# Long convolution and its two adjoints: DFTs of 1024 points in place of 1023, overlap-add on the spectra in place of a second pair of inverse matrices

## The chip, the cores and the metric

The kernel runs on one core of a Trainium2 chip. A core has a matrix engine (PE, with its weight loads shown apart as PEld), a vector engine (DVE), an activation engine (ACT), GpSimd (POOL) and a sync engine (SP), each with a queue of its own that is worked off in order, and 16 DMA engines. The metric is the time of one execution on the device in microseconds (us). A profile is one execution with its instructions recorded; its span is the time from the first to the last of them.

## What is computed

One layer, forward and backward. With `xn` the layer norm of x (2048 x 576):

```python
K = einsum("dn,dnl,dn->dl", Cc, P, dB).real           # 576 kernels of 2048 taps
y = irfft(rfft(pad(xn.T)) * rfft(pad(K)))[:, :2048]   # causal convolution along the sequence
s = y.T + xn * Dskip
g = silu(ffn(xn))                                     # gated feed-forward, 576 -> 4608 -> 576
out = x + s * g
```

The reference returns `out` and the gradients of it for x and all parameters. With gs the gradient that reaches s, the convolution's backward needs two correlations: gK (of gs with xn), from which the gradients of the parameters of K follow, and the part of xn's gradient that comes from gs and K. Output 9 is the sum over the sequence of gs * xn.

## The kernel before

The work runs in stages, one behind another in the text: constants and layer norm (phase 1), the parameters (phase 2), the generation of K (`phase2_kgen`, 36 chunks of 16 columns), the convolution (`phase3_conv`), the feed-forward (phase 4), the two correlations (`phase5_scopeA`), the sums that make the parameter gradients (`param_sums`, again 36 chunks) and the feed-forward's backward (phase 6). A framework puts every engine's instructions in order by dependencies and a priority that follows the text, so that an instruction far down in the text may be queued early where its inputs and buffers are there; it adds the semaphores. Buffers come from pools: a pool with `bufs=2` has two places for each name, and a tile waits until the one before it in its place has been read for the last time. A pool that is opened later may lie where a closed one lay, and waits for its last readers.

The sequence of 2048 is cut into NB = 4 blocks of LS = 512. A block lies as KT = 4 tiles of 128 rows by D = 576 columns, and `dpieces` cuts the columns into two of 288 for PSUM. All of the convolution is done by blocks: `fwd_dft` (L508) turns a block into a real and an imaginary spectrum of 512 frequencies with matrices `Cf` and `Sf`, 8 PSUM groups of 4 matmuls for each piece, evicted by ACT. `cmac` (L523) multiplies two block spectra on DVE and adds to an accumulator, with 6 instructions of 2304 elements for a first product and 8 for another. The DFT has M = 1023 points, so a product of two blocks of 512 fits without wrapping, and 512 frequencies hold all of it.

The inverse of output block m has two parts: the first 512 outputs of its own product sum (`CiL`, `SiL`) and the tail of the previous block's (`CiPN`, `SiPN`, kept as `Yprev` or `Znext`). A group of one output tile and one piece therefore has 16 matmuls, 8 for the block at the edge. In `phase3_body` the products are `Yr`, `Yi` from a pool with two buffers; the epilogue on DVE (L629, L631) adds xn * Dskip, and `s_t` goes to `S_dram`. The spectra of xn and K are kept in DRAM (`UH_dram`, `KH_dram`) for the backward.

`phase5_scopeA` transforms gs, forms output 9 with a column of ones, loads the spectra of xn, computes gK by four blocks from the last to the first (L871, evicted by ACT to `gK` at L872), loads the spectra of K, and computes the other correlation in the same way (L906), with an epilogue on DVE that adds gs * Dskip and a store to `GXN_dram`. `build_dft_mats` (L462) makes the six matrices from the row and column numbers on DVE and ACT; it is called twice, at the head of phase 3 and at the head of phase 5. `param_sums` begins with a copy of gK and a copy of it times the position (`gKK`, L941 and L943).

Of the kernel before, what the change touches and what calls it, by code (L numbers as in the profile page):

```python
# [10 lines left out]
ACT = mybir.ActivationFunctionType  # L11
ALU = mybir.AluOpType
# [4 lines left out]
P = 128  # L17
# [43 lines left out]
class K:  # L61
# [368 lines left out]
    def gen_dft_rows(self, sb, out_c, out_s, tvals_col, col0, ncols, wcol=None, sin_sign=-1.0):  # L430
        nc, cfg = self.nc, self.cfg
        M = float(cfg.M)
        TWO_PI_S = 6.283184
        assert ncols <= self.irow.shape[1]
        prod = sb.tile([P, ncols], FP32, name="g_prod")
        nc.vector.tensor_scalar(out=prod[:], in0=self.irow[:, 0:ncols], scalar1=float(col0), scalar2=tvals_col,
                                op0=ALU.add, op1=ALU.mult)
        q = sb.tile([P, ncols], FP32, name="g_q")
        nc.vector.tensor_scalar(out=q[:], in0=prod[:], scalar1=1.0 / M, scalar2=MAGIC, op0=ALU.mult, op1=ALU.add)
        nc.vector.tensor_scalar(out=q[:], in0=q[:], scalar1=-MAGIC, scalar2=-M, op0=ALU.add, op1=ALU.mult)  # L440
        tau = sb.tile([P, ncols], FP32, name="g_tau")
        nc.vector.tensor_tensor(out=tau[:], in0=prod[:], in1=q[:], op=ALU.add)
        u = sb.tile([P, ncols], FP32, name="g_u")
        nc.vector.tensor_scalar(out=u[:], in0=tau[:], scalar1=1.0 / M, scalar2=MAGIC, op0=ALU.mult, op1=ALU.add)
        nc.vector.tensor_scalar(out=u[:], in0=u[:], scalar1=-MAGIC, scalar2=None, op0=ALU.add)
        fr = sb.tile([P, ncols], FP32, name="g_fr")
        nc.vector.scalar_tensor_tensor(out=fr[:], in0=tau[:], scalar=1.0 / M, in1=u[:], op0=ALU.mult,
                                       op1=ALU.subtract)
        A = sb.tile([P, ncols], FP32, name="g_A")
        nc.scalar.activation(out=A[:], in_=fr[:], func=ACT.Abs)  # L450
        if wcol is None:
            nc.scalar.activation(out=out_s, in_=fr[:], func=ACT.Sin, scale=sin_sign * TWO_PI_S)
# [42 lines left out]
    def dpieces(self):  # L495
        D = self.cfg.D
        if D <= 512:
            return [(0, D)]
        n = (D + 511) // 512
        w = (D + n - 1) // n  # L500
        out = []
        o = 0
# [895 lines left out]
```

## Time and profile before

| | us |
|---|---|
| median of 3 runs | 3275.29 (3269.64 to 3278.9) |
| profiled execution | 3264.63 |
| its span | 3262.9 |
| PE busy | 2197.4 (67%) |
| DVE busy | 1750.6 (54%) |
| ACT busy | 1424.8 (44%) |
| convolution, from the last tile of K to the first matmul of phase 4 | about 401 to 657 |
| phase 4 | about 657 to 1131 |
| correlations, to the first matmul of the parameter sums | about 1131 to 1550 |
| parameter sums and their end | about 1550 to 2148 |
| phase 6 | about 2148 to 3263 |

The profile is read from a page of the whole execution and from views of its trace: groups of instructions by line, the order of time, who waited for whom, the chain of work that ended last, and windows with each engine's busy time. An engine that is busy in a window does not have to be what sets its length; an idle one that others wait for can. "PEclk" is the share of full speed at which the matrix engine was clocked.

### The profile page before, as it was taken

The numbers are of one execution on the slowest core, as the hardware profiler recorded it, in microseconds if no ns is written. First come the engines' busy times: TensorE is split into PE (matmuls) and PEld (weight loads), VectorE is DVE, ScalarE is ACT, GpSimd is POOL, SyncE is SP. The second block draws the span as 40 slices with busy tenths as digits, with TensorE's granted clock in tenths as the row PEclk, the third lists the DMA queues.
The fourth block names the chain that finished last, engine by engine and source line by source line (L and its number), as shares of the span: only waits on it lengthen the run. The fifth ranks groups of instructions, "written<-read, shape, count | busy, mean of one in ns | idle before, by whom it ended". The sixth has DMA issues, their size and how long they took to land.

```text
span 3262.9 us, 43023 instructions
## 1 busy us (share of the span) xinstructions
PE 2197.4 (67%) x17602; PEld 1417.2 (43%) x17670; DVE 1750.6 (54%) x2690; ACT 1424.8 (44%) x1626; POOL 256.0 (8%) x504
## 2 busy tenths in 40 slices
PE   1556556499979854453444444169899999956999
PEld 1232235333337633331111111047677777744777
DVE  6586847734435657678777777734343444310222
ACT  2899752044431151001777667166555555500000
POOL 0000000021111000000000000022222222110000
PEclk7555578699989967676555555589999999977999
DMA  3100011186667510110000000075444444347442
GB/s 94 29 27 23 26 58 73 43 293 222 234 227 241 153 58 5 58 58 22 14 17 14 17 17 13 13 220 169 127 139 140 130 137 132 113 116 212 170 153 84
DMA packets 311752, 333.81 MB, mean 102 GB/s; under 512 B 113833, under 2 KB 271786, under 8 KB 308354
## 3 DMA queue, kind: packets, MB, share of 16 engines
q1 hardware_dynamic: 173914, 116.20, 12.2%
q0 software_dynamic: 33552, 109.15, 10.0%
q10 hardware_dynamic: 104088, 105.71, 9.9%
q8 instruction: 138, 2.26, 0.3%
q14 instruction: 60, 0.49, 0.0%
HBM read 163.94 MB, written 150.52 MB: 96 GB/s over the span
## 4 chain that ended last, share of the span: by engine, by line
PE 29%; DVE 21%; issue 18%; ACT 7%; DMA 5%; POOL 3%; SPq 3%; ACTq 0%; POOLq 0%; DVEq 0%
PE px L1283 8%; PE ph L1190 4%; DVE pr_q L1000 3%; PE dft_ps L516 3%; SPq L1095 3%; PE pgw L1231 2%; ACT S_q L302 2%; DMA out_dram<-gw 2%; PE inv_ps L627 2%; PE pT L996 2%; DVE S_all L1002 2%; PE gk_ps L871 2%; PE pgw L1219 2%; PE gu_ps L906 2%; ACT A_q L304 2%
## 5 line engine op out<-in xcount | busy, mean ns | idle before, releaser
L1283 PE MATMUL px<-w1T,ggc 128*128 128x288 bf16 x1152 | 237.3, 288 | 42.7 <-DMA w1T<-in_B_w_dram 42.7
L1231 PEld LDWEIGHTS <-xn_bf 128*128 128x128 bf16 x2304 | 228.4, 100 | 68.9 <-issue 38.6
L1283 PE MATMUL px<-w3T,guc 128*128 128x288 bf16 x1152 | 237.2, 288 | 28.3 <-DMA guc<-GU_dram 19.7
L1000 DVE TENSOR_TENSOR pr_q<-pT,pz 128x512 f32<-128x512 f32 x144 | 146.9, 1061 | 72.0 <-PE pT L996 72.0
L1234 DVE CAST gw<-pgw 128x256 bf16<-128x256 f32 x144 | 59.9, 423 | 233.2 <-DMA out_dram<-gw 137.4
L711 DVE CAST g_t<-pg 128x1024 bf16<-128x1024 f32 x72 | 88.2, 1225 | 179.8 <-ACT s_t L710 179.8
L703 PEld LDWEIGHTS <-wmB_w 128*128 128x128 bf16 x1152 | 107.2, 98 | 159.0 <-issue 41.2
L1287 DVE TENSOR_TENSOR gx<-px,gx 128x288 f32<-128x288 f32 x32 | 13.2, 453 | 293.0 <-PE px L1283 293.0
L1300 ACT ACTIVATE t<-gx 128x576 f32<-128x576 f32 x16 | 10.9, 683 | 362.9 <-DVE gx L1287 362.9
L996 PE MATMUL pT<-gKK,qr 128*128 128x32 bf16 x576 | 69.7, 233 | 145.8 <-DVE qr L990 145.8
L1219 PE MATMUL pgw<-go_o,h_n 128*128 128x288 bf16 x1152 | 165.7, 287 | 0.8
L1231 PE MATMUL pgw<-gg_n,xn_bf 128*128 128x256 bf16 x1152 | 138.8, 283 | 35.1 <-DVE gw L1234 35.1
L1190 PE MATMUL ph<-go_oT,w2T 128*128 128x512 bf16 x682 | 161.2, 380 | 1.4 <-ACT gh L1193 0.3
L747 PE MATMUL po<-w2res,hc 128*128 128x288 bf16 x1152 | 145.8, 288 | 17.9 <-DMA hc<-H_dram 17.9
L710 ACT ACTIVATE s_t<-pg 128x1024 bf16<-128x1024 f32 x72 | 73.7, 1023 | 166.2 <-PE pu L708 154.2
L1283 PEld LDWEIGHTS <-ggc 128*128 128x128 bf16 x1152 | 113.4, 99 | 73.0 <-issue 43.8
L703 PE MATMUL pg<-xnT,wmB_w 128*128 128x512 bf16 x561 | 137.2, 382 | 8.8 <-DMA S_dram<-s_t 5.9
L1283 PEld LDWEIGHTS <-guc 128*128 128x128 bf16 x1152 | 113.3, 98 | 59.1 <-DMA guc<-GU_dram 20.2
L1231 PE MATMUL pgw<-gu_n,xn_bf 128*128 128x256 bf16 x1152 | 137.5, 273 | 0.0
L703 PE MATMUL pu<-xnT,wmB_w 128*128 128x512 bf16 x562 | 136.4, 381 | 0.7
L996 PEld LDWEIGHTS <-qr 128*128 128x128 bf16 x576 | 63.9, 122 | 167.6 <-DVE qr L990 167.6
L747 PEld LDWEIGHTS <-hc 128*128 128x128 bf16 x1152 | 112.2, 99 | 48.1 <-issue 18.4
(361 smaller groups left out, 5273.0 us busy)
## 6 DMA issues: line engine op xcount, KB each, us to landing
U_dram<-u_t POOLq DMA_DIRECT2D x36, 512.0 KB, 3.1
G_dram<-g_t POOLq DMA_DIRECT2D x36, 512.0 KB, 4.1
H_dram<-h_t SPq DMA_DIRECT2D x36, 512.0 KB
hc<-H_dram SPq DMA_DIRECT2D x8, 2304.0 KB
gate<-G_dram POOLq DMA_DIRECT2D x36, 512.0 KB, 5.4
up<-U_dram POOLq DMA_DIRECT2D x36, 512.0 KB, 6.2
GU_dram<-guT ACTq DMA_DIRECT2D x36, 512.0 KB
GG_dram<-ggT ACTq DMA_DIRECT2D x36, 512.0 KB
```

The lines of the kernel that those rows point to most:

```text
L516: nc.tensor.matmul(pt[:, 0:pw], lhsT=mat[:, tt, kc * P:(kc + 1) * P], rhs=src_fn(tt)[:, po:po + pw], start=(tt == 0), stop=(tt == KT - 1))
L703: nc.tensor.matmul(pt[:, o:o + 512], lhsT=wm[w][:, c, cs], rhs=xnT[:, c, t0:t0 + 512], start=(c == 0), stop=False)
L710: nc.scalar.activation(out=s_t[:, hs], in_=pg[:], func=ACT.Silu)
L711: nc.vector.tensor_copy(out=g_t[:, hs], in_=pg[:])
L747: nc.tensor.matmul(po_[:, pi_, 0:pw], lhsT=hc[:, fi, k * P:(k + 1) * P], rhs=self.w2res[:, fi, po:po + pw], start=(fi == 0), stop=(fi == F ...
L996: nc.tensor.matmul(pT[:, dl, k, :], lhsT=q[:, dl, :], rhs=gKK[:, :, :, d0 + dl], start=True, stop=True)
L1000: nc.vector.tensor_tensor(out=pr[:, :, kind], in0=pT[:, :, :, kind * LT:(kind + 1) * LT], in1=pz[:, s:s + 2].rearrange("p r a d -> p d r a ...
L1095: self.nc.sync.dma_start_transpose(out=dst, in_=src)
L1190: nc.tensor.matmul(ph[:, q * 512:(q + 1) * 512], lhsT=w2T[:, c, :], rhs=go_oT[:, c, hh * HL + q * 512:hh * HL + (q + 1) * 512], start=(c = ...
L1219: nc.tensor.matmul(pgw[pi_][:, 0:pw], lhsT=h_ns[fl][:, tt, :], rhs=go_o[:, tt, po:po + pw], start=(tt == 0), stop=(tt == LT - 1))
L1231: nc.tensor.matmul(pw_[:, 0:GW], lhsT=self.xn_bf[:, tt, c * P:(c + 1) * P], rhs=nat[:, tt, :], start=(tt == 0), stop=(tt == LT - 1))
L1283: nc.tensor.matmul(px[pi_][:, 0:pw], lhsT=act[:, fi, k * P:(k + 1) * P], rhs=wT[:, fi, po:po + pw], start=(fi == 0 and ai == 0), stop=(fi ...
```

## The change

The DFT gets 1024 points. The frequency 512 (Nyquist) has no imaginary part, and neither has frequency 0: so the sine slot of frequency 0 holds the Nyquist term. Both block products and inverse have to treat row 0 of that slot apart: a second version of a spectrum (`spectrum_variants`) whose imaginary row 0 is the Nyquist value and whose cross part is zero there.

With 1024 points, a shift by 512 multiplies frequency k by (-1)^k. So "this block's head plus the previous block's tail" is one inverse of a spectrum plus a sign times another. In the forward convolution and the correlation with K, that sum is made on the spectra of K once: block b's spectrum plus the sign times the previous block's (`scalar_tensor_tensor` with `sgn`, from fp32 spectra `kraw`). For gK, whose kernel side is xn, the sum is made on the result `Z`, which gives `ZZ`. `CiPN` and `SiPN` go, and every inverse group (`idft_tile`) has 8 matmuls. One cosine matrix `dC` serves both directions, and the weights of the inverse are folded into K's spectra (`hrowM`, 1/512) or the eviction.

All of it runs by column halves of 288 (`conv_half`, `conv_bwd_half`, each called twice), a complex spectrum is one tile of [P, 2, KT, 288], and one ACT instruction evicts both parts of a DFT tile. `cmul_acc` has full passes over both parts, one of them with the second operand's parts in reverse order (`B[:, ::-1]`) and `Az` broadcast over the parts, and two passes of half length. The matrices are built once, ahead of `phase2_params`, and are held until phase 5 is done. `gKK` is written by ACT straight from PSUM (two evictions a tile), and the copies on DVE go. The stores to `S_dram` and `GXN_dram` are half as wide, and all are issued by ACT; loads are issued by SP.

```diff
     def build_dft_mats(self, pool):
...
+            for tt in range(KT):
+                tcol = sb.tile([P, 1], FP32, name=f"dft_t{tt}")
+                nc.vector.tensor_scalar(out=tcol[:], in0=self.pcol[:], scalar1=float(tt * P), scalar2=None, op0=ALU.add)
+                nc.vector.tensor_scalar(out=fr[:, tt, :], in0=self.irow[:, 0:LS], scalar1=tcol[:, 0:1], scalar2=None,
+                                        op0=ALU.mult)
+            nc.vector.tensor_scalar(out=q[:], in0=fr[:], scalar1=1.0 / M, scalar2=MAGIC, op0=ALU.mult, op1=ALU.add)
+            nc.vector.tensor_scalar(out=q[:], in0=q[:], scalar1=-MAGIC, scalar2=None, op0=ALU.add)
+            nc.vector.scalar_tensor_tensor(out=fr[:], in0=fr[:], scalar=1.0 / M, in1=q[:], op0=ALU.mult,
+                                           op1=ALU.subtract)
+            nc.scalar.activation(out=self.dSf[:], in_=fr[:], func=ACT.Sin, scale=-6.283184)
+            nc.scalar.activation(out=q[:], in_=fr[:], func=ACT.Abs)
+            nc.scalar.activation(out=self.dC[:], in_=q[:], func=ACT.Sin, scale=-6.283184, bias=self.halfpi_col[:])
+            nc.vector.tensor_copy(out=self.dSi[:], in_=self.dSf[:])
...
+    def dft_block(self, ps, src_fn, dst, scale=None):
+        for kt in range(KT):
+            pt = ps.tile([P, 2, 512], FP32, name="dft_ps")
+            for ri, mat in enumerate((self.dC, self.dSf)):
+                for tt in range(KT):
+                    nc.tensor.matmul(pt[:, ri, 0:W], lhsT=mat[:, tt, kt * P:(kt + 1) * P], rhs=src_fn(tt),
+                                     start=(tt == 0), stop=(tt == KT - 1))
+            if scale is None:
+                nc.scalar.copy(out=dst[:, :, kt, :], in_=pt[:, :, 0:W])
...
+    def spectrum_variants(self, A2, Az):
+        nc.vector.tensor_copy(out=A2[:, 1], in_=A2[:, 0])
+        nc.vector.tensor_copy(out=A2[0:1, 1, 0, :], in_=Az[0:1, 0, :])
+        nc.vector.memset(Az[0:1, 0, :], 0.0)
+
+    def cmul_acc(self, acc, A2, Az, B, tp, first, conj):
+        if first:
+            tt_(out=acc[:], in0=A2[:], in1=B[:], op=ALU.mult)
         else:
+            t1 = tp.tile([P, 2, KT, W], BF16, name="cm_t")
+            tt_(out=t1[:], in0=A2[:], in1=B[:], op=ALU.mult)
+            tt_(out=acc[:], in0=acc[:], in1=t1[:], op=ALU.add)
+        t2 = tp.tile([P, 2, KT, W], BF16, name="cm_t")
+        tt_(out=t2[:], in0=B[:, ::-1], in1=Az[:, None].to_broadcast([P, 2, KT, W]), op=ALU.mult)
+        tt_(out=acc[:, 0], in0=acc[:, 0], in1=t2[:, 0], op=ALU.add if conj else ALU.subtract)
+        tt_(out=acc[:, 1], in0=acc[:, 1], in1=t2[:, 1], op=ALU.subtract if conj else ALU.add)
...
+        with self.tc.tile_pool(name="c_k", bufs=1) as kp, \
+                self.tc.tile_pool(name="c_u", bufs=1) as up, \
+                self.tc.tile_pool(name="c_raw", bufs=2) as rp, \
+                self.tc.tile_pool(name="c_y", bufs=2) as ypool, \
+                self.tc.tile_pool(name="c_tmp", bufs=2) as tp, \
...
+            for h in range(2):
+                self.conv_half(h, kp, up, rp, ypool, tp, spool, ps, ps2)
...
+        for b in range(NB):
+            kr = rp.tile([P, 2, KT, W], FP32, name="kraw")
+            self.dft_block(ps, lambda tt: self.KT[:, b * KT + tt, cs], kr, scale=1.0 / 512)
...
+                nc.vector.scalar_tensor_tensor(out=k2[:, 0], in0=prev[:, 0], scalar=self.sgn[:, 0:1], in1=kr[:, 0],
+                                               op0=ALU.mult, op1=ALU.add)
+                nc.vector.scalar_tensor_tensor(out=kz[:], in0=prev[:, 1], scalar=self.sgn[:, 0:1], in1=kr[:, 1],
+                                               op0=ALU.mult, op1=ALU.add)
...
+        for m in range(NB):
+            u = up.tile([P, 2, KT, W], BF16, name=f"u_{m}")
+            self.dft_block(ps, lambda tt: self.xn_bf[:, m * KT + tt, cs], u)
+            nc.sync.dma_start(out=self.UH_dram[h, m], in_=u[:])
+            V = ypool.tile([P, 2, KT, W], BF16, name="V")
+            for i in range(m + 1):
+                self.cmul_acc(V, K2[i], Kz[i], U[m - i], tp, i == 0, False)
+            for oc in range(KT):
+                pt = ps2.tile([P, 512], FP32, name="inv_ps")
+                self.idft_tile(pt, V, oc)
...
+        with self.tc.tile_pool(name="b_k", bufs=1) as kp, \
+                self.tc.tile_pool(name="b_g", bufs=1) as gp, \
+                self.tc.tile_pool(name="b_gs", bufs=2) as gsp, \
+                self.tc.tile_pool(name="b_z", bufs=3) as zp, \
...
+        for i in range(NB - 1, -1, -1):
+            Z = zp.tile([P, 2, KT, W], BF16, name="Z")
+            for k, m in enumerate(range(i, NB)):
+                self.cmul_acc(Z, A2[m - i], Az[m - i], G[m], tp, k == 0, True)
+            if nxt is not None:
+                ZZ = zp.tile([P, 2, KT, W], BF16, name="ZZ")
+                nc.vector.scalar_tensor_tensor(out=ZZ[:], in0=nxt[:], scalar=self.sgn[:, 0:1], in1=Z[:], op0=ALU.mult,
+                                               op1=ALU.add)
...
+                nc.scalar.activation(out=gKK[:, 0, t, cs], in_=pt[:, 0:W], func=ACT.Copy, scale=1.0 / 512)
+                nc.scalar.activation(out=gKK[:, 1, t, cs], in_=pt[:, 0:W], func=ACT.Copy, scale=self.lcol[:, t:t + 1])
...
+        for j in range(NB):
+            Z = zp.tile([P, 2, KT, W], BF16, name="Z")
+            for k, i in enumerate(range(NB - j)):
+                self.cmul_acc(Z, A2[i], Az[i], G[i + j], tp, k == 0, True)
...
-            gKK = big.tile([P, 2, LT, D], BF16, name="gKK")
-            nc.vector.tensor_copy(out=gKK[:, 0], in_=gK[:])
-            for t in range(LT):
-                nc.vector.tensor_scalar(out=gKK[:, 1, t, :], in0=gK[:, t, :], scalar1=self.lcol[:, t:t + 1], scalar2=None,
-                                        op0=ALU.mult)
...
         k.phase1_layernorm()
+        mats = ExitStack()
+        k.build_dft_mats(mats.enter_context(tc.tile_pool(name="mats", bufs=1)))
         k.phase2_params()
```

More of the change, by code (lines that the diff above doesn't have):

```diff
@@ new lines, in dpieces @@
+        return [(0, D // 2), (D // 2, D // 2)]
+    def dft_block(self, ps, src_fn, dst, scale=None):
+        nc, KT = self.nc, self.cfg.KT
+        W = self.cfg.D // 2
+        for kt in range(KT):
[6 more added lines that the diff above has]
+                nc.scalar.copy(out=dst[:, :, kt, :], in_=pt[:, :, 0:W])
+            else:
+                nc.scalar.activation(out=dst[:, :, kt, :], in_=pt[:, :, 0:W], func=ACT.Copy,
+                                     scale=self.hrowM[:, 0:1] if kt == 0 else scale)
```

467 lines of the change are left out of this document (147 added, 320 removed).

## The prediction

> **What bounds the kernel now.** I read the page's chain first, to see whether one engine carries the span.
>
> ```profile
> PE 29%; DVE 21%; issue 18%; ACT 7%; DMA 5%; POOL 3%; SPq 3%; ACTq 0%; POOLq 0%; DVEq 0%
> ```
>
> None does: the chain changes between engines, so a change is priced stage by stage. The view by windows gives the stages that the edit touches; its columns are named in its first row.
>
> ```profile
> core 0: us, PE busy (x) PEld busy (x) DVE busy (x) ACT busy (x) POOL busy (x), PEclk, DMA share, GB/s
> 401.00:447.00 46.00, 3.18 (x8) 0.78 (x9) 43.92 (x103) 21.14 (x36) 0.00 (x0) 0.50 0.00 0
> 447.00:525.00 78.00, 76.67 (x531) 52.19 (x531) 28.52 (x27) 50.02 (x127) 0.00 (x0) 0.96 0.27 109
> 525.00:657.00 132.00, 57.11 (x424) 42.81 (x423) 94.82 (x109) 1.68 (x2) 5.89 (x8) 0.72 0.16 56
> 1131.00:1188.00 57.00, 14.00 (x51) 4.46 (x49) 53.92 (x135) 25.19 (x44) 0.00 (x0) 0.54 0.28 101
> 1188.00:1226.00 38.00, 37.46 (x248) 24.86 (x246) 0.72 (x1) 24.68 (x62) 0.00 (x0) 0.93 0.00 1
> 1226.00:1374.00 148.00, 65.53 (x448) 47.62 (x449) 97.88 (x74) 12.39 (x32) 0.00 (x0) 0.70 0.11 35
> 1374.00:1528.00 154.00, 65.38 (x448) 47.54 (x447) 118.00 (x130) 0.35 (x1) 0.00 (x0) 0.70 0.12 40
> ```
>
> 401 to 447 and 1131 to 1188 are the two builds of the DFT matrices: DVE is full, PE all but idle. 447 to 525 and 1188 to 1226 are forward DFTs: PE full, DVE near idle. In the other three DVE does the spectral products and PE the inverse DFTs, and little of that lies side by side (65.53 + 97.88 = 163 in a window of 148): they take turns. The chain in order of time shows the turns, and the view of waits who waits for whom.
>
> ```profile
> 1250.88 1.37 DVE Zi L559
> 1252.29 16.76 PE gk_ps L871 x125
> ...
> 1356.02 17.54 PE gk_ps L871 x123
> ...
> 1414.94 2.57 DMA GXN_dram<-gx
> ...
> 1510.61 17.42 PE gu_ps L906 x126
> 1528.51 2.46 DVE gKK L941
> 1530.97 4.46 DVE gKK L943 x16
> ```
>
> ```profile
> PE inv_ps L627 <- DVE Yr L538: 58.9, 2, 35.0
> DVE Zr L545 <- PE gk_ps L871: 48.1, 3, 16.4
> ```
>
> Each block's inverse (8 groups of 16 matmuls) takes about 17 us with DVE waiting. The cause is in the code: the inverse of block m reads the previous block too, the pool has two buffers, so the products of the next block have no buffer until it ends.
>
> **The change, part by part.** The ends between which it acts:
>
> ```profile
> 400.42 0.42 DVE L426 CAST KT<-kps 128x256 bf16<-128x256 f32 x1 [0.49 <-PE kps L424]
> 656.73 0.58 PE L703 MATMUL pg<-xnT,wmB_w 128*128 128x512 bf16 x1 [5.92 <-DMA S_dram<-s_t]
> 1127.17 4.22 PE L747 MATMUL po<-w2res,hc 128*128 128x288 bf16 x33
> 1550.43 0.22 PE L996 MATMUL pT<-gKK,qi 128*128 128x32 bf16 x1 [0.87 <-DVE qi L990]
> 47.14 0.06 DVE L176 MEMSET logdt_bf<- 128x5 bf16 x1 [12.61 <-DMA XNT_dram<-xnT_bf]
> 52.83 0.82 DVE L224 TENSOR_TENSOR rho<-A_re_bf,dt_col 128x640 f32<-128x640 bf16 x1 [0.95 <-ACT dt_col L214]
> 94.19 0.59 PE L397 MATMUL t_ps<-SEL,lhs_t 128*128 128x512 bf16 x1 [27.28 <-DMA lhs_r<-PCS_dram]
> ```
>
> Forward convolution: 400.8 to 656.7, 256 us. Adjoints up to the first matmul of the parameter sums: 1131.4 to 1550.4, 419 us. Prices of instructions, from the groups by form and the timeline:
>
> ```profile
> L559 DVE TENSOR_TENSOR Zi<-Zi,ztmp 128x2304 bf16<-128x2304 bf16 x12 | 16.3, 1358 | 0.4
> L415 DVE TENSOR_TENSOR t_k<-p_k,WrT 128x1024 bf16<-128x1024 bf16 x36 | 24.7, 686 | 0.4
> L447 DVE SCALAR_TENSOR_TENSOR g_fr<-g_tau,g_u 128x512 f32<-128x512 f32 x16 | 10.9, 682 | 0.0
> L340 DVE SCALAR_TENSOR_TENSOR val<-dl,pm,val 128x1536 f32<-128x1536 f32 x1 | 1.8, 1815 | 0.0
> L941 DVE COPY gKK<-gK 128x9216 bf16<-128x9216 bf16 x1 | 2.5, 2548 | 0.0
> L912 DVE TENSOR_TENSOR gx<-gu_ps,gx 128x288 f32<-128x288 f32 x32 | 14.4, 455 | 30.8 <-PE gu_ps L906 30.6
> L302 ACT ACTIVATE S_q<-m_q,npi_col 128x2048 bf16<-128x2048 int32 x36 | 71.8, 1994 | 20.6 <-DVE m_q L984 20.6
> L752 ACT ACTIVATE sgo<-po 128x576 f32<-128x576 f32 x16 | 10.4, 650 | 69.4 <-issue 48.4 <-PE po L747 21.0
> 449.44 1.16 PE L516 MATMUL dft_ps<-KT,Cf 128*128 128x288 bf16 x4
> 450.40 1.16 PE L516 MATMUL dft_ps<-KT,Sf 128*128 128x288 bf16 x4
> 637.41 0.29 PE L627 MATMUL inv_ps<-Yr,CiL 128*128 128x288 bf16 x1
> 637.53 0.29 PE L627 MATMUL inv_ps<-Yi,SiL 128*128 128x288 bf16 x1
> ```
>
> A matmul of 288 columns issues every 0.96/4 = 0.24 us while PE is slow (0.50 granted) and every 0.12 us when fast.
>
> *Products.* An entry of the convolution has 10 complex products, 4 first and 6 accumulating. Before: 4 x 6 + 6 x 8 = 72 passes of 2304 elements, at 1.36 us, 98 us a stage. After, over both column halves: 8 first ones (2 full passes, 2 of half length) and 12 others (3 full, 2 half) make 52 full and 40 half passes; a half pass is 1.36/2 + 0.04 = 0.72 us. 52 x 1.36 + 40 x 0.72 = 100 us a stage, 50 a column half. So DVE's product work is not cut. New is one operand with its two parts reversed, and one broadcast over the two parts. L415 has a broadcast operand and still streams two elements a cycle (1024 in 0.69 us); no row shows a reversed one. Nothing: 0, or the price of L340's pace, 1.24 us more a pass. I take 0, as innermost rows stay contiguous in both.
>
> *Inverse.* The second pair of matrices goes: 448 matmuls become 256 per stage, 8 in a group, and nothing reads the previous block any more. So products of the next block run beside this block's inverse. What is late next is DVE itself. On gK, DVE gets the sign sum instead: 3 scalar_tensor_tensor of 2304 per half. Its pace from L447 to L340 is 1.13/1024 us an element, so 2.6 us each; as a packed pass it would be 1.36. I take 2.6, the only kind of row there is (6 x 1.24 = 7 us in doubt). With a copy (0.8) and four 576-element scalings (0.36, as L943's 4.46/16 with its start) that is 10 us a half.
>
> The Trainium skill, Vector Engine (DVE) Microarchitecture Reference, section 5.1, lists copy, cast, tensor_scalar and tensor_tensor as the ops with packed modes, which leaves scalar_tensor_tensor at one element a cycle; it also says that streaming with a negative step was not measured. By it the 2.6 holds, and the reversed pass stays open.
>
> *Forward stage, summed.* (a) No build at 401: K's DFTs start at once. A block is 32 matmuls, first at 0.24 us (7 us with its eviction), then paced by two raw fp32 buffers: two sign sums of 1152 on DVE (1.4 us each), two evictions (0.65), two DFT tiles (1.0 each) make about 6.4 us a block. 7 + 19 and U's first DFT (4): 30 us to the first product. (b) Half 0 on DVE: 50 + 16 x 2 x 0.455 = 64.6. (c) K of half 1 on DVE: per block 2.8 and variants 0.75 (a 1152 copy 0.47 by L941's pace, two one-row ops), 13 in all, and 6 of waiting for raw buffers. (d) Half 1: 64.6. (e) The last inverse: 32 x 0.24 = 8. Sum 186 against 256: **-70 us**.
>
> *Adjoints, summed.* (a) The matrices are there, so G's DFTs start when the last forward matmul ends: 4 blocks of 36 matmuls at 0.12 us, 18, and 3 for the last gradient tile's way through DRAM: 21. (b) Half 0: 100 for both products, 10 for the sign sums, 14.6 for gx, less 7 that falls in the gap: 118. (c) Between halves every buffer is single: the last spectrum of G is read until the last product, and gs has two buffers, so load (2.6 us, as GXN's DMA on the chain) and DFT (4) run mostly one behind the other for four blocks: 24 us. (d) 118. (e) 16 to the first parameter matmul: before it was 13 from the end of gKK at 1535.4 + 2, and pool space now comes free with the last inverse. The 8.3 us of DVE for gKK go to ACT as 32 more evictions, each under L752's 0.65 us (of 576 elements), beside DVE. Sum 297 against 419: **-122 us**.
>
> *The moved build.* Once, in 47 to 94: DVE 4 x 0.48 + 2 x 1.2 + 2.4 + 0.7 + 14 tiny ones x 0.15 = 9.5; ACT 3 x 2.0 and a table load 1.3. DVE stands from 47.1 to 52.8 waiting for loads and covers about 5. Behind it on DVE stand the rate pieces whose DMAs gate the first matmul at 94. Bounds 0 and 13 (if ACT's Exp and its load issues stand behind the sines); **+5 us**. Its 12 KB stay resident through phase 4; the streams there keep their buffers: 0.
>
> Sum: -70 - 122 + 5 = -187. 3262.9 - 187 = 3076 of span; the profiled execution took 3264.6 (1.7 around its span), the median of the runs is 3275.3, 10.7 above. On the median's footing: 3088, which I round to 3085.
>
> **Rivals.** (1) *No bubbles.* The scheduler fills the gap and the K waits with other work: (c) of the adjoints falls to 5, forward (a) and (c) lose 12, the sums start 9 earlier; 40 us less: 3045. For it: instructions far ahead in the text already run early in idle slots. Against: the single buffers.
> (2) *The reversed pass runs at one element a cycle.* 20 of them a stage, 60 in all, 1.24 us each: 74 us, 3160. For: no row excludes it. Against: contiguous rows.
> (3) *PE stays slow and binds.* At 0.24 us forward half needs 384 x 0.24 = 92 us of PE against DVE's 78; +28 us for both, 3113. For: windows with gaps have 0.70. Against: they rise to 0.93 when DFTs follow each other. The Trainium skill, TensorE: Matmul & The Clock Gate, "HAM oscillation", says that idle gaps over some 3.4 us return PE to half clock; fewer matmuls beside the same DVE work make such gaps likelier. By it this rival holds for the inverses, less for the DFTs.
> (4) *The turns stay.* If the order on DVE puts a block's epilogue ahead of the next products, DVE waits for each of 24 half-block inverses, 4 to 8 us: 24 x 5 = 120, 3205. For: engines take their queues in order. Against: early runs as above.
> (5) *Slower: all product passes lose the packed mode* through their shapes with two parts: 3 x (52 x 1.24 + 40 x 0.62) = 268 us, 3353. It decides from a mean of 2.2 us a full pass instead of 1.36 (187 us over 216 full-pass equivalents). L415 speaks against it.
>
> **How the numbers follow.** Forecast 0.48, (1) 0.17, (2) 0.12, (3) 0.12, (4) 0.08, (5) 0.03. The range 3025 to 3165 takes in the forecast, (1), (2), (3) and the bounds of the build (-5 to +8) and sign sum (-7); (4) and (5) are left out, 0.11 with some of the edges. All but (5) are faster by more than 0.3% (10 us, about what these runs can tell from no change): 0.96, same 0.01, slower 0.03.
>
> **What would show it.** Right: the two stages have DVE busy over 80%, PE's waits for products are short, product passes stay at 1.36 and 0.72 us, the first forward matmul of phase 4 comes some 186 us after K, the first parameter matmul some 297 us after phase 4. Wrong: a product pass near 2.6 us (2 or 5), DVE waiting for inverse groups (4), granted clock 0.5 with PE full (3), a start of kgen later than 107, or a stage outside the convolutions that grows: I give these nothing.

## The result, and the profile after

The changed kernel takes 3080.25 us (median of 4 runs, 3078.52 to 3081.98) against 3274.01 (4 runs, 3269.64 to 3278.9): a ratio of 0.9408, 95% interval 0.9392 to 0.9424. The forecast was 3085, in a range of 3025 to 3165.

The points between which the change acts, in the order of time of the profile after (columns: start and duration in us, engine, line, operation; in brackets the idle time before it and what ended it):

```profile
50.08 0.15 DVE L448 TENSOR_SCALAR hrow<-pcol 128x1 f32<-128x1 f32 x1 [12.73 <-DMA XNT_dram<-xnT_bf]
64.57 0.06 DVE L176 MEMSET dskip_bf<- 128x5 bf16 x1 [2.31 <-ACT dC L466]
109.31 0.59 PE L397 MATMUL t_ps<-SEL,lhs_t 128*128 128x512 bf16 x1 [26.00 <-DMA lhs_r<-PCS_dram]
415.08 0.42 DVE L426 CAST KT<-kps 128x256 bf16<-128x256 f32 x1 [1.97 <-PE kps L424]
592.04 0.58 PE L653 MATMUL pg<-xnT,wmB_w 128*128 128x512 bf16 x1 [11.39 <-issue]
599.52 3.57 PE L653 MATMUL pu<-xnT,wmB_w 128*128 128x512 bf16 x8 [3.91 <-DMA wmB_w<-in_B_w_dram]
1065.24 4.22 PE L697 MATMUL po<-w2res,hc 128*128 128x288 bf16 x33
1083.29 0.90 PE L485 MATMUL dft_ps<-gs,dC 128*128 128x288 bf16 x3 [7.93 <-DMA gs<-GS_dram]
1373.45 0.21 PE L902 MATMUL pT<-gKK,qi 128*128 128x32 bf16 x1 [1.03 <-DVE qi L896]
1886.15 0.23 PE L902 MATMUL pT<-gKK,qr 128*128 128x32 bf16 x1
```

The last matmul of the parameter sums in the kernel before, from the same view:

```profile
2062.44 0.23 PE L996 MATMUL pT<-gKK,qr 128*128 128x32 bf16 x1
```

With the rows that the prediction shows of before, the two spans divide into the same six stretches. The table is of the two profiled executions: that of before took 3264.63 us, 9.4 less than its median, and that of after 3080.9, 0.65 more than its own. So the spans differ by 183.8 us where the medians differ by 193.8.

| stretch | before | after | change | forecast |
|---|---|---|---|---|
| start to the last tile of K | 400.8 | 415.5 | +14.7 | +5 |
| forward convolution, to the first matmul of phase 4 | 255.9 | 176.5 | -79.4 | -70 |
| phase 4 | 474.7 | 477.4 | +2.8 | 0 |
| correlations, to the first matmul of the parameter sums | 419.0 | 304.0 | -115.1 | -122 |
| parameter sums | 512.2 | 512.9 | +0.7 | 0 |
| from there to the end | 1200.2 | 1192.7 | -7.5 | 0 |
| span | 3262.9 | 3079.1 | -183.8 | -187 |

The windows of the two stages, cut at the first and last product of each half (columns in the first row):

```profile
core 0: us, PE busy (x) PEld busy (x) DVE busy (x) ACT busy (x) POOL busy (x), PEclk, DMA share, GB/s
415.50:441.60 26.10, 21.75 (x151) 16.04 (x151) 13.86 (x24) 12.62 (x20) 3.34 (x6) 0.88 0.42 151
441.60:497.00 55.40, 34.63 (x269) 26.13 (x268) 55.31 (x71) 13.08 (x21) 0.00 (x0) 0.88 0.20 76
497.00:518.90 21.90, 18.24 (x119) 12.88 (x118) 15.32 (x30) 7.84 (x12) 0.00 (x0) 0.84 0.35 135
518.90:574.70 55.80, 26.23 (x188) 19.09 (x187) 55.39 (x70) 7.67 (x12) 4.05 (x7) 0.76 0.26 90
574.70:592.00 17.30, 5.93 (x30) 3.71 (x29) 2.29 (x5) 0.00 (x0) 4.25 (x6) 0.70 1.04 362
1069.50:1104.60 35.10, 21.46 (x149) 14.38 (x150) 12.54 (x29) 12.00 (x20) 0.00 (x0) 0.81 0.44 127
1104.60:1216.50 111.90, 46.00 (x225) 28.57 (x225) 110.41 (x121) 12.85 (x32) 0.00 (x0) 0.66 0.25 74
1216.50:1241.20 24.70, 22.97 (x175) 16.20 (x175) 10.29 (x29) 10.55 (x17) 0.00 (x0) 1.00 0.35 98
1241.20:1353.00 111.80, 46.10 (x225) 28.82 (x225) 110.29 (x121) 12.85 (x33) 0.00 (x0) 0.66 0.18 55
1353.00:1373.40 20.40, 12.81 (x50) 4.64 (x49) 16.61 (x26) 9.91 (x12) 0.00 (x0) 0.77 0.13 41
```

The four windows of products have DVE busy for 55.31 of 55.40, 55.39 of 55.80, 110.41 of 111.90 and 110.29 of 111.80 us: the turns are gone and DVE sets the length. Of the other six, 1216.50 to 1241.20, between the halves of the correlations, has PE all but full (22.97 of 24.70 us, at a granted clock of 1.00), and 574.70 to 592.00 has the DMA engines full, with a share of 1.04; in the rest nothing is.

The waits show the same from the other side (who waited for whom, us in all, times, longest). The first two lines are of the forward stage after, between 410 and 600, the third of the correlations after, between 1104 and 1353, and the last of the forward stage before, between 400 and 657:

```profile
PE inv_ps L501 <- DVE V L525: 49.4, 8, 17.2
DVE s_t L588 <- PE inv_ps L501: 4.2, 5, 1.9
DVE gx L826 <- PE inv_ps L501: 1.8, 4, 0.9
DVE s_t L631 <- PE inv_ps L627: 27.5, 24, 3.8
```

PE now waits for the products. DVE waits for the inverses 4.2 us in the forward stage, where it was 27.5, and 1.8 us in the correlations, where the line in the prediction has 48.1 for gK alone.

Prices of instructions after, from the groups by form (count, then busy time in us and mean in ns):

```profile
L524 DVE TENSOR_TENSOR cm_t<-g,az 128x2304 bf16<-128x2304 bf16 x40 | 53.9, 1348 | 0.0
L521 DVE TENSOR_TENSOR cm_t<-a,g 128x2304 bf16<-128x2304 bf16 x24 | 32.4, 1348 | 0.0
L525 DVE TENSOR_TENSOR Z<-Z,cm_t 128x1152 bf16<-128x1152 bf16 x40 | 30.0, 750 | 0.3
L795 DVE SCALAR_TENSOR_TENSOR ZZ<-Z,sgn 128x2304 bf16<-128x2304 bf16 x6 | 15.7, 2609 | 0.0
```

L524 is the pass with reversed parts and a broadcast operand; it takes what the plain pass of L521 takes, 1348 ns. L525 is a pass of half length, and L795 the sign sum.

### The profile page after: what moved, and what is told of

Its sections match the earlier page's. It is cut to its first block, busy times and chain, and to the rows that moved or that the text cites. A ratio compares the mean times of both kernels' runs of the same rounds, so it can differ in the third digit from the quotient of the medians.

```text
span 3079.1 us, 41743 instructions
## 1 busy us (share of the span) xinstructions
PE 2130.0 (69%) x17026; PEld 1366.9 (44%) x17094; DVE 1698.6 (55%) x2604; ACT 1387.4 (45%) x1493; POOL 256.2 (8%) x505
## 4 chain that ended last, share of the span: by engine, by line
PE 23%; DVE 16%; issue 8%; ACT 6%; DMA 6%; SPq 3%; POOL 2%; ACTq 0%; POOLq 0%; DVEq 0%
PE px L1189 9%; PE ph L1096 4%; DVE pr_q L906 4%; SPq L1001 3%; DMA out_dram<-gw 3%; PE pgw L1137 3%; ACT S_q L302 2%; PE pT L902 2%; DVE S_all L908 2%; PE pgw L1125 2%; ACT A_q L304 2%; DVE m_q L890 1%; DVE cm_t L524 1%; PE ptr L1009 1%; DMA w2T<-w2r 1%
## 5 line engine op out<-in xcount | busy, mean ns | idle before, releaser
L1125 PE MATMUL pgw<-go_o,h_n 128*128 128x288 bf16 x1152 | 164.9, 286 | 0.9
L660 ACT ACTIVATE s_t<-pg 128x1024 bf16<-128x1024 f32 x72 | 73.8, 1024 | 162.6 <-PE pu L658 162.6
```

The source lines that it names most:

```text
L660: nc.scalar.activation(out=s_t[:, hs], in_=pg[:], func=ACT.Silu)
L1125: nc.tensor.matmul(pgw[pi_][:, 0:pw], lhsT=h_ns[fl][:, tt, :], rhs=go_o[:, tt, po:po + pw], start=(tt == 0), stop=(tt == LT - 1))
```

## The experiments

Each ratio is to the kernel before, run on the same chip; the changed kernel stands at 0.9408. "Less" and "more" are against its median of 3080.25. Two things limit how finely they can be read. The median of the kernel before itself lay between 3272.06 and 3277.39 in the sets of runs, so a few us of each difference are uncertain. And the stretch behind the parameter sums, which no edit here touches, lasted between 1184 and 1193 us in the profiled executions of the changed kernel and of the ten runs that start from it; what moves there can't be put down to an edit.

**1. Room for the build's scratch (e1_room).** In the profile after, a memset of the parameters waits at 64.57 for ACT's dC, the last reader of the scratch of the matrix build.

```diff
-        with self.tc.tile_pool(name="dftgen", bufs=1) as sb:
+        with self.tc.tile_pool(name="dftgen", bufs=1, side="right") as sb:
```

> The changed kernel, but the scratch of the matrix build lies at the other end of the memory, so that no later pool lies where it lay. Theory (placement): the parameter tiles waited for the last reader of that scratch, ACT's dC; with room of its own the parameter loads start as early as in the kernel before, the first matmul of kgen comes at 95 to 100 us in place of 109.3, and the time is 3066 to 3071 (10 to 14 us less). Rival (queue order): the build's own work on DVE (9.5 us) and ACT (7.3 us) stands ahead of the parameters' in their queues wherever its scratch lies; the first matmul stays at 107 to 110 and the time within 3 us of 3080.

Measured: 3073.59 (4 runs, 3070.71 to 3074.89), 0.9375 (0.9362 to 0.9389), 6.7 us less. In the order of time of this run:

```profile
49.79 0.15 DVE L446 CAST sgn<-dft_pb 128x1 f32<-128x1 int32 x1 [12.54 <-DMA XNT_dram<-xnT_bf]
...
103.07 1.95 PE L397 MATMUL t_ps<-SEL,lhs_t 128*128 128x512 bf16 x4 [28.14 <-DMA lhs_r<-PCS_dram]
```

The first matmul of kgen comes 6.2 us earlier: placement is less than half of the 15 us. Neither theory has it alone, and both ranges are missed.

**2. The build behind the parameters (e11_late).** The same, with the build put behind `phase2_params` in the text.

```diff
-        k.build_dft_mats(mats.enter_context(tc.tile_pool(name="mats", bufs=1)))
+        mp = mats.enter_context(tc.tile_pool(name="mats", bufs=1))
         k.phase2_params()
+        k.build_dft_mats(mp)
```

> The changed kernel with the build's scratch in room of its own and the build put behind the parameters in the text. Room alone moved kgen's first matmul from 109.3 to 103.1; the kernel before, and the run with the two builds in place, had it at 94 to 96. Theory (the other 8 us are the queue order: the build's 9.5 us on DVE and 7.3 us on ACT stand ahead of the parameters): the first matmul comes at 95 to 98 and the time is 3064 to 3068. Rival (the build then stands ahead of kgen's first chunk, or the 8 us are the memory that the resident matrices take): first matmul or last tile of K no earlier than with room alone, 3071 to 3076.

Measured: 3069.46 (5 runs, 3063.89 to 3072.67), 0.9375 (0.9362 to 0.9389). The time is 1 us above the theory's range, and the first matmul 2 us later than its range. From the order of time of this run:

```profile
53.75 0.06 DVE L176 MEMSET dskip_bf<- 128x5 bf16 x1 [13.25 <-DMA XNT_dram<-xnT_bf]
...
100.26 4.94 PE L397 MATMUL t_ps<-SEL,lhs_t 128*128 128x512 bf16 x9 [27.50 <-DMA lhs_r<-PCS_dram]
```

DVE's stand ends with the layer norm's last store: at 47.14 before, 50.08 after, 49.79 and 53.75 in these two runs. From there to the first matmul it is 47.1 us before, 59.2 after, 53.3 with room, 46.5 here. So the build cost 12.2 us after that store: 5.9 by where its scratch lay, the rest by its place in the queues; with both mended it costs nothing there. But the store itself comes 2.9 us later after the change, and 6.6 here, which is why the time hardly falls. The order of time on DVE shows where that comes from. In the changed kernel a cast of the parameters stands in the middle of the layer norm and waits for its load; in the kernel before it came behind the layer norm:

```profile
9.07 0.17 DVE L186 CAST logdt_f<-logdt_bf 128x5 f32<-128x5 bf16 x1 [2.62 <-DMA logdt_bf<-in_A_log_dt_dram]
```

With room (run 1) that cast doesn't wait, but DVE does the large passes of the build there, 6.4 us, in place of 3.7 us of work for kgen, and the store is 2.7 us later than before. In this run there are both, the wait and the build's passes. So what is taken out of the parameters' way lands partly in the layer norm, where it delays what stands behind it on DVE.

**3. The matrices built twice, in place (e2_twice).** The call at the head goes, and both stages build their three matrices as the kernel before built its six.

```diff
-        k.build_dft_mats(mats.enter_context(tc.tile_pool(name="mats", bufs=1)))
...
+            with tc.tile_pool(name="mats", bufs=1) as mp:
+                k.build_dft_mats(mp)
+                k.phase3_conv()
...
+            with self.tc.tile_pool(name="mats", bufs=1) as mp:
+                self.build_dft_mats(mp)
+                self.phase5_conv_bwd(gKK)
```

> The changed kernel, but the three matrices are built where the kernel before built its six: at the head of the convolution and again at the head of the correlations. Theory (the build of three is cheap wherever it stands): each build puts about 17 us in the path, as at the start of the changed kernel, and the start gets its 15 us back: 3080 + 34 - 15 = about 3099 (3090 to 3110). Rival (building once and early is worth what the two builds took before, 46 and 57 us): 3080 + 103 - 15 = about 3168.

Measured: 3080.55 (4 runs, 3069.09 to 3084.72), 0.9392 (0.9371 to 0.9414): no change that these runs can tell. Both theories missed. The profiled execution is the fastest of the four, 11 us under their median. The windows of this run from the last tile of K, and from the last matmul of phase 4, to the first product, and its first matmul of phase 4 in the order of time:

```profile
402.60:443.40 40.80, 24.10 (x168) 17.79 (x169) 20.20 (x36) 18.82 (x23) 0.00 (x0) 0.77 0.17 66
1056.30:1096.30 40.00, 23.05 (x149) 15.23 (x150) 21.00 (x53) 19.00 (x24) 0.13 (x1) 0.74 0.37 111
```

```profile
587.24 1.89 PE L653 MATMUL pg<-xnT,wmB_w 128*128 128x512 bf16 x8 [3.80 <-DMA S_dram<-s_t]
```

They are 40.80 and 40.00 us long where the changed kernel has 26.10 and 35.10: two builds in place cost 14.7 + 4.9, some 20 us. They are paid for elsewhere: kgen's first matmul comes at 95.95 in place of 109.31, phase 4 begins 9.8 us after the last product in place of 17.3, and lasts 469 us in place of 477. In this execution that is more than the builds cost; by the medians the two are equal. That the build is made once and early is thus worth nothing that shows here; the last two numbers led to the next run.

**4. The loads of w2res (e5_w2sp).** POOL's and SP's issues at the head of phase 4 of the changed kernel, from the order of time:

```profile
572.25 5.94 POOL L638 DMA_DIRECT2D w2res<-in_B_w_dram  x8 [42.83 <-DVE cm_t L524]
```

```profile
573.07 4.21 SPq L633 DMA_DIRECT2D wmB_w<-in_B_w_dram  x2
```

Eight loads of 576 KB, for matmuls that begin at 912, leave POOL just ahead of the first weights.

```diff
-                    nc.gpsimd.dma_start(out=self.w2res[:, fi:fi + GRP, :],
+                    nc.sync.dma_start(out=self.w2res[:, fi:fi + GRP, :],
```

> The changed kernel with the loads of w2res (9 of 576 KB) issued by SP, behind the first weights of phase 4, in place of POOL. Theory (a stream that was let go ahead: with the matrices resident, eight of these loads leave POOL's queue at 572, before the first weights, which then land at 592 and 599): the first matmul of phase 4 comes about 10 us after the last product in place of 17, phase 4 itself takes 469 us in place of 477, together 15 us less, 3063 to 3068. Rival (the stretch is set by the last stores of the convolution or by the smaller room that the resident matrices leave): within 4 us of 3080.

Measured: 3059.91 (4 runs, 3058.18 to 3063.01), 0.9337 (0.9325 to 0.935), 20 us less. From the order of time of this run:

```profile
584.75 2.30 PE L653 MATMUL pg<-xnT,wmB_w 128*128 128x512 bf16 x8 [3.98 <-DVE s_t L588]
586.84 3.21 PE L653 MATMUL pu<-xnT,wmB_w 128*128 128x512 bf16 x8
```

Phase 4 begins 10.1 us after the last product, its second group no longer waits for a weight, and it lasts 471.4 us to the last matmul, at 1056.2. The theory holds for these 13 us; another 5 came behind the parameter sums, which it doesn't explain and which puts the time 3 us below its range. The DMA engines are as full as before in the window from 574.70 to 584.75 (share 1.06): what changed is which load goes first.

**5. A third product buffer in the kernel before (e3_before3).** Six matrices, two builds and 16 matmuls a group stay. For the room, the pool of the second stage is opened behind that of gs.

```diff
-                self.tc.tile_pool(name="c_y", bufs=2) as ypool, \
+                self.tc.tile_pool(name="c_y", bufs=3) as ypool, \
...
-                    self.tc.tile_pool(name="b_z", bufs=2) as zpool, \
...
+                zpool = zst.enter_context(self.tc.tile_pool(name="b_z", bufs=3))
```

> The kernel before with three buffers in place of two for the products of both stages; six matrices, two builds, 16 matmuls a group. Theory (most of the gain of the product and inverse part came from ending the turns between DVE and PE, not from fewer matmuls): the stretch from 525 to 657 shrinks towards DVE's 95 us and that from 1226 to 1528 towards DVE's 216 us; with the short first blocks still bound by their inverses, some 80 to 105 us less, 3170 to 3195. Rival (the queue order keeps the turns, or the 16 matmuls a group bind next): within 20 us of 3274.

Measured: 3191.93 (4 runs, 3185.73 to 3193.71), 0.9734 (0.9719 to 0.9749): 85 us less than the kernel before. The first matmuls of phase 4 and of the parameter sums, and the last one of phase 4, in the order of time of this run:

```profile
635.53 1.86 PE L703 MATMUL pg<-xnT,wmB_w 128*128 128x512 bf16 x4 [5.75 <-DMA S_dram<-s_t]
1106.84 4.22 PE L747 MATMUL po<-w2res,hc 128*128 128x288 bf16 x33
1468.36 0.22 PE L998 MATMUL pT<-gKK,qi 128*128 128x32 bf16 x1 [0.87 <-DVE qi L992]
```

With K's last tile done at 402.7, the forward stage takes 232.8 us (23 less than before), the correlations 357.3 (62 less). So of the 194 us that the change gains in the two stages, 85 can be had in the old code by one more buffer in two pools, one of them opened later.

**6. Sixteen matmuls a group (e4_16mm).** Every inverse group of the changed kernel is run through twice.

```diff
-        n = 2 * KT + len(extra)
+        n = 4 * KT + len(extra)
...
-        for kt in range(KT):
+        for kt in [*range(KT), *range(KT)]:
```

> The changed kernel with every inverse group run through twice (16 matmuls in place of 8, 768 more in all; what it sums is doubled). Theory (DVE is the bound and PE is hidden beside it): only the inverses that nothing covers grow, those at the end of the two halves of each stage and beside the short first products: 20 to 40 us more, 3100 to 3120. Rival (the halving of the matmuls was what mattered): 768 matmuls at 0.12 to 0.24 us, 92 to 184 us more, 3172 to 3264.

Measured: 3098.88 (4 runs, 3092.85 to 3107.11), 0.9462 (0.9442 to 0.9482), 18.6 us more for 768 matmuls. Windows of this run, over both halves' products and the gap in the forward stage, and over the products of each half in the correlations:

```profile
442.00:589.30 147.30, 106.45 (x797) 80.43 (x796) 127.84 (x168) 28.50 (x45) 3.97 (x7) 0.87 0.23 83
1119.00:1228.70 109.70, 64.05 (x419) 45.56 (x419) 109.05 (x118) 12.85 (x33) 0.00 (x0) 0.78 0.25 73
1259.80:1369.00 109.20, 62.22 (x420) 44.59 (x420) 108.89 (x119) 12.82 (x32) 0.00 (x0) 0.80 0.18 54
```

The forward stretch from the first product to the last takes 147.3 us in place of 133.1, and DVE waits for inverses there 10.7 us in place of 0.5. In the correlations the products take 109.7 and 109.2 us, no more than the 111.9 and 111.8 of the changed kernel; the gap between them is 31.1 in place of 24.7, and PE is full there (30.30 us). So PE is hidden beside the products of the correlations, but neither in the gap nor beside the first blocks of the forward stage, whose products are too short to cover it. The cost is just under the theory's range, far from the rival's.

**7. The sign sum shared with ACT (e8_zz).**

```diff
-                nc.vector.scalar_tensor_tensor(out=ZZ[:], in0=nxt[:], scalar=self.sgn[:, 0:1], in1=Z[:], op0=ALU.mult,
-                                               op1=ALU.add)
+                nc.scalar.activation(out=ZZ[:], in_=nxt[:], func=ACT.Copy, scale=self.sgn[:, 0:1])
+                nc.vector.tensor_tensor(out=ZZ[:], in0=ZZ[:], in1=Z[:], op=ALU.add)
```

> The changed kernel with the sign sum of gK split: ACT writes the sign times the neighbour's spectrum, DVE adds in a packed pass (1.27 us) in place of the 2.6 us pass. Theory (DVE is the bound of the stage, microsecond for microsecond): six times 1.3 us, 7 to 8 us less, 3071 to 3074. Rival (another engine or a queue sets the pace of gK, or ACT's 2 us pass comes late because it stands behind the evictions): within 2 us of 3080, or slower.

Measured: 3073.07 (4 runs, 3068.24 to 3074.74), 0.9374 (0.9361 to 0.9387), 7.2 us less. From its groups by form:

```profile
L795 ACT ACTIVATE ZZ<-Z,sgn 128x2304 bf16<-128x2304 bf16 x6 | 13.3, 2215 | 23.6 <-DVE Z L526 23.6
L796 DVE TENSOR_TENSOR ZZ<-ZZ,Z 128x2304 bf16<-128x2304 bf16 x6 | 8.1, 1358 | 0.0
```

Six passes of 2.61 us have become six of 1.36: 7.5 us taken from DVE, 7.2 from the time by the medians, and 9.4 from the correlations in the profiled execution (294.6 us in place of 304.0). In these stretches DVE is the path.

**8. Load order and buffers of the correlations (e6_corr).**

```diff
-        with self.tc.tile_pool(name="b_k", bufs=1) as kp, \
+        with self.tc.tile_pool(name="b_k", bufs=2) as kp, \
-                self.tc.tile_pool(name="b_gs", bufs=2) as gsp, \
-                self.tc.tile_pool(name="b_z", bufs=3) as zp, \
+                self.tc.tile_pool(name="b_gs", bufs=4) as gsp, \
+                self.tc.tile_pool(name="b_z", bufs=2) as zp, \
-                self.tc.tile_pool(name="b_s", bufs=3) as sp, \
+                self.tc.tile_pool(name="b_s", bufs=5) as sp, \
...
+        GSL = []
+        for b in range(NB):
+            gs = gsp.tile([P, KT, W], BF16, name="gs")
+            nc.sync.dma_start(out=gs[:], in_=self.GS_dram[:, b * KT:(b + 1) * KT, cs])
+            GSL.append(gs)
...
```

> The changed kernel; in the correlations the loads of gs stand ahead of those of xn's spectra in the text and have four buffers, the spectra of the loaded side two, the epilogue five in place of three; the products have two in place of three for the room. Theory (single buffers and load order make the gap between the halves and the late start): the gap falls from 24.8 us to 6 to 10 (only the last spectrum of G is still held until the last product), the start from 35 to about 29, some 22 us less, 3055 to 3062. Rival (the gap is what G's DFTs take on PE, 4 times 4 us, and two product buffers bring the turns back): gap stays at 20 to 25, 3075 to 3100.

Measured: 3072.72 (5 runs, 3064.14 to 3073.43), 0.9375 (0.9362 to 0.9388), 7.5 us less. The window of the gap in this run, and SP's issues at the start of the correlations in the order of time:

```profile
1224.50:1236.80 12.30, 8.60 (x65) 5.54 (x63) 8.05 (x21) 2.59 (x5) 0.00 (x0) 1.00 0.63 199
```

```profile
1073.37 0.33 SPq L774 DMA_DIRECT2D a<-UH_dram  x1
...
1083.75 2.02 SPq L767 DMA_DIRECT2D gs<-GS_dram  x4
```

The gap halves, 24.7 to 12.3: PE has 65 matmuls left in it in place of 175, as most DFTs of the second half's gs now run beside the first half's products, and DVE has 8.05 us of its own work there. The profiled execution is the fastest of the five, 8.6 us under their median; in it the correlations are 11.4 us shorter, and 9 us more lie behind the parameter sums. The start doesn't shrink: it goes from 35.1 to 37.4 (last matmul of phase 4 ending at 1073.3, first product at 1110.7). Text order did not put gs first in SP's queue; the eight loads of the spectra are still ahead of it. That half of the theory was not tested by this edit.

**9. More buffers in the forward stage (e7_fwd).**

```diff
-        with self.tc.tile_pool(name="c_k", bufs=1) as kp, \
+        with self.tc.tile_pool(name="c_k", bufs=2) as kp, \
-                self.tc.tile_pool(name="c_s", bufs=3) as spool, \
+                self.tc.tile_pool(name="c_s", bufs=6) as spool, \
```

> The changed kernel with two buffers for K's spectra and six for the epilogue in the forward stage. Theory (DVE waits in the gap because K's spectra of the second half find no free place until the first half's last product): DVE keeps the 13 us of K's work, the 9 us of waiting go, 3070 to 3073. Rival (the raw fp32 spectra, still two, pace it): the gap stays at 22 us, within 3 us of 3080.

Measured: 3077.88 (4 runs, 3075.3 to 3079.85), 0.9391 (0.9378 to 0.9403): no change that these runs can tell. The gap stays at 23 us, so the theory falls, but the rival's reason isn't the one that the trace shows. ACT in the order of time:

```profile
472.32 0.65 ACT L490 ACTIVATE kraw<-dft_ps 128x576 f32<-128x576 f32 x1 [0.33 <-PE dft_ps L485]
...
505.96 0.74 ACT L490 ACTIVATE kraw<-dft_ps,hrowM 128x576 f32<-128x576 f32 x1 [32.99 <-DMA S_dram<-s_t]
```

ACT had begun on the second half's spectra at 465, in the middle of the first half's products, and then stood 33 us at its own store issues: each waits for an epilogue that DVE has queued among its products, and the evictions stand behind it. In the changed kernel itself a stand of 32.7 us at the same place ends when DVE's `kz` frees a raw buffer, as the rival has it; so either can hold ACT there.

**10. The stores by POOL (e9_fwdq).** The same, with three raw buffers, and the stores on a queue that has nothing else to do there.

```diff
-                nc.scalar.dma_start(out=self.S_dram[:, t, cs], in_=s_t[:])
+                nc.gpsimd.dma_start(out=self.S_dram[:, t, cs], in_=s_t[:])
```

> The changed kernel with two buffers for K's spectra, three for the raw ones, six for the epilogue, and the stores to S_dram issued by POOL in place of ACT. Theory (in the run with more buffers alone, ACT stood 33 us behind its own store issues, which wait for DVE's epilogues, so that the evictions of K's second half came late): the gap between the two halves' products falls from 22.6 us to the 13 us of DVE's work for K, 9 us less, 3069 to 3073. Rival (PE's order or DVE's own order puts K's second half there anyway): gap over 20 us, within 3 us of 3078.

Measured: 3059.04 (5 runs, 3054.22 to 3063.44), 0.9342 (0.9325 to 0.9359), 21 us less. The window of the gap in this run:

```profile
491.60:506.40 14.80, 13.02 (x87) 9.35 (x86) 13.98 (x26) 5.13 (x8) 2.15 (x4) 0.83 0.46 178
```

DVE is busy for 13.98 of 14.80 us: the waiting is gone. The forward stage takes 164.9 us from K's last tile (416.0 to 581.0) in place of 176.5, about what was expected and 2 more, as K's first half is shorter too. The edit frees ACT from the stores and gives it a third raw buffer at once; how the gain divides between the two is not shown. Some 9 us more came behind the parameter sums, where nothing was edited; why is open.

**11. Together (e10_all).** Runs 1, 4, 7, 8 and 10 in one kernel.

> Together: scratch of the build with room of its own, w2res by SP, the sign sum split between ACT and DVE, the reordered loads and buffers of the correlations, and the forward stage with buffers and stores by POOL. Theory (separate stretches of one path, so the savings add up): 7 + 20 + 7 + 8 + 9 = 51 us less than 3080, 3025 to 3035. Rival (they share the same waits: the loads that come earlier meet other transfers): less than two thirds of it, over 3045.

Measured: 3027.57 (4 runs, 3024.1 to 3032.76), 0.925 (0.9234 to 0.9266), 53 us less than the changed kernel, as the theory has it. It is not the whole sum, though: the five runs measured 6.7, 20.3, 7.2, 7.5 and 21.2 us less, 63 together. In the stretches that the edits touch, the profiled executions of the five runs add to 51 us, and this run has 46; the difference is in the correlations, 14.9 us shorter where runs 7 and 8 had 9.4 and 11.4.

## Why the prediction was right, and where it was not

**Products unchanged, reversed pass at full pace.** Right. The pass with the reversed operand takes 1348 ns like the others; rivals (2) and (5) fall with it. The half pass was put at 0.72 us and takes 0.75. Passes that don't wait for each other start every 1.27 us (1104.61, 1105.88 and 1107.15 in the correlations), where a chain in the kernel before, each pass waiting for the one ahead, had 1.39; so the product windows are shorter than the sums: 111.9 for 118 in the correlations.

**The sign sum at 2.6 us.** Right, 2609 ns for 2304 elements. The Trainium skill's Vector Engine (DVE) Microarchitecture Reference, section 5.1, leaves this operation out of those with packed modes; the trace agrees.

**The turns go, and DVE is late next.** Right: DVE is over 98% busy in the four windows of products, and run 7 takes its saving off the time. Rival (4) falls, and so does rival (1), as the gap of the correlations stays at 24.7 us where that rival has 5. Run 5 prices the turns alone at 85 us. One reading was wrong, without effect on the sum: in 447 to 525 of the kernel before DVE was not near idle but busy for 28.52 of 78 us.

**Fewer matmuls, PE hidden.** Right, and run 6 prices it: 18.6 us for twice the matmuls. Rival (3) had its condition met in part, as PE was granted 0.66 in the products of the correlations, but with 46 us of PE beside 112 of DVE that binds nothing. PE sets the pace only in the gap between the halves, step (c) below. The Trainium skill's TensorE: Matmul & The Clock Gate, "HAM oscillation", expects the lower clock from the idle gaps, and the trace agrees: PE stands for up to 16.3 us at a time there. In run 6, with more of the gaps filled, the same windows have 0.78 and 0.80.

**The forward stage, -70; it was -79.4.** Step by step: (a) 26.1 for 30; (b) and (d) 55.4 and 55.8 for 64.6, as passes are closer together and the last block's epilogues fall behind the window; (c) 21.9 for 19; (e) 17.3 for 8. The last is mis-sized for a cause that the prediction had ruled out, below.

**The adjoints, -122; it was -115.1.** (a) 35.1 for 21: the prediction gave 3 us to the last gradient tile's way through DRAM, and PE's first DFT matmul came 13.8 us after phase 4's last one, at 1083.29, waiting for the load of gs. (b), (d) 111.9 and 111.8 for 118. (c) 24.7 for 24, but this agreement is luck: the loads and the DFTs of gs did not run one behind the other. PE finished the last inverse at 1221.5, a part that (c) left out, and then ran the four blocks' DFTs without a stop until 1240.5, 4.7 us a block for the 4 that were forecast, with the loads beside them. That single buffers kept those DFTs out of the first half was right: run 8 shows that they made half of (c). (e) 20.4 for 16.

**"The moved build: +5", with bounds 0 and 13.** Wrong: 14.7. The step that failed is "DVE stands from 47.1 to 52.8 waiting for loads and covers about 5". Those loads don't run beside the build: they wait for its last reader, since their tiles lie where its scratch lay (run 1, 6 us), and the build stands ahead of them in the queues (run 2, the rest of 12). The remaining 3 are the layer norm's later store, behind a cast that waits in its middle.

**"Its 12 KB stay resident through phase 4; the streams there keep their buffers: 0".** Wrong. The buffers stayed, but the stream of w2res was let go ahead of the first weights, and in the window from 574.70 to 592.00 the DMA engines were full (share 1.04). It cost 7 us in step (e) and 6 in phase 4 (run 4). In the kernel before, the first weights left SP at 632.00, 19 us ahead of w2res (651.11) and 25 ahead of the first matmul; in the changed one both left together (573.07 and 572.25). Whether the residence alone did this is not shown; with the matrices built in place (run 3) w2res left at 584.21, behind the weights (575.85).

**The sum.** -194 of the two stages against a forecast of -192, +15 against +5 at the start, +3 in phase 4, and -7.5 behind the parameter sums that nothing predicted and no run explains: the total, 3 us off in the span, owes something to misses of both signs. The step from the span to the median was wrong too: it added 10.7 us because the profiled execution of before lay that far under its median, and the one of after does not (3080.9 against 3080.25). Without it the forecast would have been 3078. By the runs, the 194 us are about 85 for the turns (run 5), 103 for the two builds that no longer stand in the stages, of which 83 come from the build of three being so much lighter than that of six (run 3), and a rest of 6 in which fewer matmuls and more work on DVE meet. Added up like this they are an account, not a measurement: the three were not undone together.

## What to carry to other kernels

Where two engines take turns, try one more buffer before a new algorithm; here that alone gave 85 of 194 us. What is moved out of a stage has a second price where it lands: in the place of its scratch, in the queues, and in what its memory sets free or holds back. After such a change look for issues that stand on a compute engine's queue behind late data, and for large loads that run ahead of small urgent ones; mending these, with the build's scratch, the buffers of the correlations and the sign sum, was worth another 53 us.

## What the runs showed of the hardware that was not expected

- A bf16 operand read with its two parts in reverse order, with the other operand broadcast over the parts, streams as fast as a plain one: 2304 elements in 1348 ns for both.
- Packed passes of 1.35 us that don't depend on each other start 1.27 us apart.
- Twice the inverse matmuls beside the same work of DVE raised the granted clock of the correlations' products from 0.66 to 0.78 and 0.80, so PE was busy for 64 and 62 us in place of 46, less than in proportion (419 and 420 matmuls for 225).
- The DMA engines were full (share 1.00 to 1.06) for some 30 us at the head of phase 4; about half of the 10 MB that they moved there were loads whose first reader starts 340 us later.
